# Strassen for the output projection of six token tiles, and a residual added by accumulating DMA

## The chip, the cores and the metric

One core of a Trainium2 chip. The metric is the device time of one execution in microseconds (us). Executions of one kernel lie within about 0.3% of their median, so each time is the median of several. Engines: PE is TensorE, VectorE, ScalarE and GpSimd are the other compute engines, SyncE (SP in the profile) only issues DMAs. The granted clock is the share of TensorE's full clock that its throttle let through.

## The reference, cut to what matters

A linear-attention layer and a gated feed-forward layer, 2048 tokens of width 1024, bf16:

```python
def _A_ref(x, wqkv, wo):                      # attention
    ...                                       # q, k, v; phi; kv, z
    o = num / den                             # "division": numerators over denominators
    return (lambda x, *d: x.transpose(*d))(o, 0, 2, 1, 3).reshape(B, S, D) @ wo   # output projection

h  = x + _A_ref(_layernorm(x, axis=-1), A_wqkv, A_wo)          # the residual that the change moves
h2 = h + _B_ref(_layernorm(h, axis=-1), B_W_gate, B_W_up, B_W_down)
```

The kernel handles tokens in 16 tiles of 128. Only the projection `@ wo` and the `x +` ahead of it are changed.

## The kernel before

A helper records every operation, and a step `t` of the stage projects tile t - 4, computes the numerators of tile t and divides them. The parts that matter:

```python
def a2_div(st):                         # VectorE: division of tile st, 128x1024
    ...                                 # two small operations for 1 / denominator
    PL.add("dve", lambda e: e.tensor_tensor(out=osb[:, k, :]..., in0=nv[:, :, :, 0:Dh], in1=rden[...], op=ALU.mult), ...)
    dma_t(sl_to[kt], oT[:, kt, :, :], osb[:, k, :], "T3d_%d" % st, ...)   # SyncE: DMA transpose for the projection

def a4_mm(st):                          # PE: 16 matmuls, 128x512 each, into one of two bank pairs
    ...
def a4_h(st):                           # VectorE: h = x + projection, then stored by SyncE
    PL.add("dve", lambda e: e.tensor_tensor(out=hsb[:, hs, :], in0=ps[:, b:b + 2, :], in1=x2(st)..., op=ALU.add), ...)
    if TPP <= st and st + NX2 < NST:
        load_x2(st + NX2)
    dma(sl_hs[hs], ov[st * P:(st + 1) * P, :], hsb[:, hs, :], "st_h_%d" % st, ...)
    ...                                 # tiles 0 to 7 (TPP = 8): statistics of the second norm
def a4_norm(st):                        # tiles 0 to 7: ScalarE normalises, SyncE transposes (T5d)
    PL.add("act", lambda e: e.activation(out=xn[:, kx, :], in_=hsb[:, hs, :], func=ACTF.Identity, ...), ...)
    dma_t(sl_tx[kx], hnT[:, :, st * P:(st + 1) * P], xn[:, kx, :], "T5d_%d" % st, ...)

pool_t = t_sums(0, "pool")              # GpSimd: eight 128x512 sums of feed-forward weights
for t in range(NE, NST + LAG + 1):
    if LAG <= t < NST + LAG: a4_mm(t - LAG)
    if t < NST: a2_num(t); a2_div(t)
    if LAG <= t < NST + LAG: a4_h(t - LAG)
    if LAG + 1 <= t < TPP + LAG + 1: a4_norm(t - LAG - 1)
    if t in (5, 7, 18, 19): load_w_next()
    if t >= 9: run(pool_t, 1)
    if 15 <= t < 19: s_sums()[t - 15]()   # VectorE: 128x2048 sums of feed-forward weights
```

Two DMA transposes matter: **T3d**, from the division to the projection of the same tile, and **T5d**, from the second norm to the feed-forward. Both are issued by SyncE, in the order in which the program records them.

Of the kernel before, what the change touches and what calls it, by code (L numbers as in the profile page):

```python
# [6 lines left out]
ALU = mybir.AluOpType  # L7
# [125 lines left out]
def bass_sequential_preLN__linear_attn_block__glu_gated_reglu__prompt_kernel(  # L133
# [15 lines left out]
    _, S, D = A_x.shape  # L149
# [56 lines left out]
    with es:  # L206
# [67 lines left out]

        osb = RE[:, 0:NO * D].rearrange("p (a b) -> p a b", a=NO)
        oT = RE[:, NO * D:(NO + NOT) * D].rearrange("p (a g t) -> p a g t", a=NOT, g=NG)
        ftmp = RE[:, 0:(NO + NOT) * D].bitcast(f32).rearrange("p (a b) -> p a b", b=SBW)
        c22 = RE[:, 2 * D:3 * D].rearrange("p (a b) -> p a b", b=SBW)
        c12 = RE[:, 3 * D:4 * D].rearrange("p (a b) -> p a b", b=SBW)
# [42 lines left out]
        Et = RX[:, 0:NPH * NW].rearrange("p (a b) -> p a b", a=NPH)  # L322
        ajunk = RX[:, 0:D]
        btmp = RX[:, NPH * NW:(NPH + 4) * NW].bitcast(f32).rearrange("p (a b) -> p a b", a=2)

        def TWq(j):
            if j < 2:
# [36 lines left out]
        def slots(name, n):  # L364
            return [_Slot(sem("%s%d" % (name, i))) for i in range(n)]
# [19 lines left out]
        sl_out2 = slots("dou2_", STB)  # L385
        sl_fin = slots("dfin_", STB)
        sl_tx = slots("dtx_", NXN)
        sl_to = slots("dto_", NOT)
        sl_hs = slots("dhs_", NHS)
        sl_hl = slots("dhl_", 2)  # L390
        sl_xl = slots("dxl_", 2)
# [2 lines left out]
        def bufs(name, n):  # L394
            return [_Buf("%s%d" % (name, i)) for i in range(n)]
# [20 lines left out]
        B_dt = bufs("dt_", NDT)  # L416
        B_rd = bufs("rd_", NDT)
        B_oT = bufs("oT_", NOT)
        B_x2 = bufs("x2_", TPP + NX2)
        B_hs = bufs("hs_", NHS)  # L420
        B_hscr = bufs("hscr_", NST)
# [48 lines left out]
        def flat(x):  # L470
            return [b for row in x for b in (flat(row) if isinstance(row, list) else [row])]
# [8 lines left out]
            b_.over = B_TWk  # L480
        for b_ in B_f + B_c22 + B_c12:
            b_.over = B_o + B_oT
        for b_ in B_hl + B_xl:
            b_.over = B_x2[TPP:]
        for b_ in flat(B_T):
            b_.over = B_wq
        for b_ in B_S:
# [23 lines left out]
        for b_ in B_hres + B_ds:  # L511
            b_.over = B_lsum
        for b_ in B_outst:
            b_.over = B_E + B_bt + [B_TWq[2], B_junk]
        for b_ in B_hnE:
            b_.over = B_o + B_oT
        for b_ in B_V:
            b_.over = B_hnE
        for b_ in flat(B_hh) + B_out2:
            b_.over = flat(B_xnT) + flat(B_pqT)  # L520
        for b_ in flat(B_pqT):
            b_.over = flat(B_wkv)
        B_TWq[3].over = [B_zeros]
# [8 lines left out]
        def touch_bank(b):  # L532
            bank_clock[0] += 1
            bank_last[b] = bank_clock[0]
# [33 lines left out]
        def dma_t(slot, dst_ap, src_ap, name, reads=(), writes=()):  # L568
            return PL.add("sp", lambda e: e.dma_start_transpose(dst_ap, src_ap), reads=reads, writes=writes,
                          slot=slot, name=name)  # L570
# [193 lines left out]
        def mm(out_ap, lhsT, rhs, start, stop, reads, bbuf, name, skip=False):  # L764
            return PL.add(
                "pe",
                lambda e: e.matmul(out_ap, lhsT, rhs, start=start, stop=stop, skip_group_check=skip),  # L767
                reads=reads, writes=[bbuf], name=name,
            )
# [433 lines left out]
        NB = [0, 1, 2, 3]  # L1203
        NUW = Dh + 2

        def a2_num(st):
            r, i, t = st // (NST // 2), (st % (NST // 2)) // 2, st % 2
            for b_ in NB:
                touch_bank(b_)
            for g in range(NG):  # L1210
                for h in range(HPG):
                    sl = slice(h * Dh, (h + 1) * Dh)
                    mm(ps[:, NB[h], g * NUW:g * NUW + Dh + 1], pqT[sl, r, t, g, i * P:(i + 1) * P],
                       kvz[sl, g, 0:Dh + 1], True, True, [B_pqT[r][t][g]] + B_kvz, B_bank[NB[h]],
                       "num_%d_%d" % (st, g), skip=True)

        def a2_div(st):
            k = st % NO
            kd = st % NDT
            kt = st % NOT  # L1220
            rb = [B_bank[b_] for b_ in NB]
            nv = ps[:, 0:HPG, 0:NG * NUW].rearrange("p h (g w) -> p g h w", w=NUW)
            PL.add("dve", lambda e: e.tensor_scalar(
                out=dtmp[:, kd, :].rearrange("p (g h) -> p g h", h=HPG), in0=nv[:, :, :, Dh],
                scalar1=1e-6, scalar2=None, op0=ALU.add), reads=rb, writes=[B_dt[kd]], name="dtmp_%d" % st)
            PL.add("dve", lambda e: e.reciprocal(out=rden[:, kd, :], in_=dtmp[:, kd, :]),  # L1226
                   reads=[B_dt[kd]], writes=[B_rd[kd]], name="rden_%d" % st)
            PL.add("dve", lambda e: e.tensor_tensor(  # L1228
                out=osb[:, k, :].rearrange("p (g h e) -> p g h e", h=HPG, e=Dh),
                in0=nv[:, :, :, 0:Dh],  # L1230
                in1=rden[:, kd, :].rearrange("p (g h) -> p g h", h=HPG).unsqueeze(3).to_broadcast([P, NG, HPG, Dh]),
                op=ALU.mult), reads=rb + [B_rd[kd]], writes=[B_o[k]], name="o_%d" % st)
            dma_t(sl_to[kt], oT[:, kt, :, :], osb[:, k, :], "T3d_%d" % st, reads=[B_o[k]], writes=[B_oT[kt]])

        H_PAIRS = [4, 6]

        a4_bank = {}

        def a4_mm(st):
            k = st % NOT  # L1240
            b = a4_bank[st] = min(H_PAIRS, key=lambda b: max(bank_last[b], bank_last[b + 1]))
            for nt in range(ND2):
                touch_bank(b + nt)
                for ct in range(NG):
                    mm(bank(b + nt, NW), oT[:, k, ct, :], wo[:, ct, nt * NW:(nt + 1) * NW],
                       ct == 0, ct == NG - 1, [B_oT[k], B_wo[nt]], B_bank[b + nt], "a4_%d_%d" % (st, nt))

        def a4_h(st):
            xs = x2_slot(st)
            hs = st % NHS  # L1250
            b = a4_bank.pop(st)
            PL.add("dve", lambda e: e.tensor_tensor(out=hsb[:, hs, :], in0=ps[:, b:b + 2, :],  # L1252
                                                    in1=x2(st).rearrange("p (a c) -> p a c", a=2), op=ALU.add),
                   reads=[B_bank[b], B_bank[b + 1], B_x2[xs]], writes=[B_hs[hs]], name="h_%d" % st)
            if TPP <= st and st + NX2 < NST:
                load_x2(st + NX2)
            dma(sl_hs[hs], ov[st * P:(st + 1) * P, :], hsb[:, hs, :], "st_h_%d" % st, reads=[B_hs[hs]],
                writes=[B_hscr[st]])
            if st >= TPP:
                return  # L1260
            ks = st % 2
            a4_k[st] = ks
            src = hsb[:, hs, :]
            junk = ajunk
            for f_ in act_stats(src, [B_hs[hs]], junk, B_junk, s2[:, ks, 0:4], B_s2[ks], "ln2_%d" % st):
                f_()
            m_, r_, n_ = s2[:, ks, 0:1], s2[:, ks, 2:3], s2[:, ks, 4:5]
            PL.add("pool", lambda e: e.tensor_scalar(out=n_, in0=m_, scalar1=r_, scalar2=-1.0, op0=ALU.mult,
                                                     op1=ALU.mult),
                   reads=[B_s2[ks][0], B_s2[ks][2]], writes=[B_s2[ks][4]], name="lnn_%d" % st)  # L1270

        a4_k = {}

# [741 lines left out]
        for p in range(NP_):  # L2015
# [5 lines left out]
            if p + 2 < NP_:  # L2021
# [25 lines left out]
                        twq.pop(0)()  # L2047
                v_group(p + 2, {2: v2, 3: v3, 5: v5, 6: v6})
        assert not twq and not twv and not twk
        for i in range(ND2):  # L2050
            load_wo(i)
        NE = 4
        for r in range(2):
            for ct in range(NG // 2):
                hooks = {}
                if r == 0 and ct == 0:
                    hooks[7] = lambda: kvaccs(NP_ - 1)
                if r == 0 and ct == 1:
                    kvc = kvfin()
                if r == 0 and ct >= 1:  # L2060
                    for h_ in (1, 3, 4, 7):
                        if kvc:
                            hooks[h_] = kvc.pop(0)
                if r == 1:
                    hooks[6] = lambda t=ct: a2_num(t)
                q_group(r, ct, hooks)
                if r == 1:
                    pend[1].insert(2 if ct + 1 < NG // 2 else 0, lambda t=ct: a2_div(t))
                if r == 0 and ct == 0:
                    for i in range(TPP + NX2):  # L2070
                        load_x2(i)
        flush()
        LAG = NOT
        pool_t = t_sums(0, "pool")
        for t in range(NE, NST + LAG + 1):
            if LAG <= t < NST + LAG:
                a4_mm(t - LAG)
            if t < NST:
                a2_num(t)
                a2_div(t)  # L2080
            if LAG <= t < NST + LAG:
                a4_h(t - LAG)
            if LAG + 1 <= t < TPP + LAG + 1:
                a4_norm(t - LAG - 1)
            if t in (5, 7, 18, 19):
                load_w_next()
            if t >= 9:
                run(pool_t, 1)
            if 15 <= t < 19:
                s_sums()[t - 15]()  # L2090
        load_w_next()
        load_w_next()
        for q in range(NWR):
# [158 lines left out]
```

## Time and profile before

| | before |
|---|---|
| median of 3 | 726.51 us (725.54 to 727.18) |
| span in the profile, granted clock | 723.5 us, 1.00 |
| third tile of the stage (tile 2) starts | 177.21 us |
| first feed-forward matmul | 229.75 us |
| the **stretch** between these two | 52.54 us |

(One of the recorded expectations calls the tile at 177.21 us the second; two tiles start before it.) The stretch is the measure by stage that I use below: all that the change can move lies in it or at the program's end, and the first 177 us vary a little from execution to execution. In timelines, columns are start, length, engine, line, operation, and output <- input. Most lines that bound the kernel are in the prediction. One view that it doesn't show is the timeline of SyncE's queue, here for the kernel before; columns are start, length, engine, line, operation, and output <- input. `RE<-RE` is a T3d, `RH<-RXH` a T5d, `out_dram<-RXH` a store.

```profile
208.63 1.30 SPq L569 DMA_TRANSPOSE RH<-RXH  x1
210.04 1.27 SPq L569 DMA_TRANSPOSE RE<-RE  x1
...
213.32 1.29 SPq L569 DMA_TRANSPOSE RH<-RXH  x1
214.72 1.50 SPq L569 DMA_TRANSPOSE RE<-RE  x1
```

Issuing a transpose keeps SyncE for 1.3 us or more, and the entries follow each other almost without a pause. The transposes at 210.04 and 214.72 are those of tiles 12 and 13. Tile 13's division ended at 210.29 (start 209.06, 1.23 us), so its transpose was issued 4.4 us after its data were ready. Direct projection has enough distance (four tiles) to hide that.

### The profile page before, as it was taken

What the parts mean: (1) busy time and instruction counts of PE and PEld (TensorE: products, weight loads), DVE (VectorE), ACT (ScalarE), POOL (GpSimd) and SP (SyncE); (2) the same over time, 40 slices, a digit from 0 to 9 for tenths busy, and PEclk for the clock granted to TensorE, in tenths of its full rate; (3) what the DMA queues carried; (4) which work ended last, traced back from release to release, by engine and by line L of the source; (5) the groups of instructions that cost most, each with busy time, mean ns of one, the idle gap of its engine ahead of it and who ended that gap; (6) DMA issues with size and microseconds to landing.
All of it is one profiled execution on the core that took longest, in us unless ns stands there. A gap on an engine that the chain in (4) does not pass through costs nothing.

```text
span 723.5 us, 12104 instructions
## 1 busy us (share of the span) xinstructions
PE 717.1 (99%) x4521; PEld 384.6 (53%) x4521; DVE 587.2 (81%) x1024; ACT 361.0 (50%) x632; POOL 109.5 (15%) x177
## 2 busy tenths in 40 slices
PE   9999999999999999999999999999999999999998
PEld 4444444344444444444444568865555555547887
DVE  7878867799776889888988787787889877887984
ACT  4878666764841456687757111035455545423010
POOL 1411100000360103322321002310000000000331
PEclk9999999999999999999999999999999999999999
DMA  9652244023998897999999999994555572037996
GB/s 316 207 115 61 37 131 156 13 29 68 195 229 258 245 267 228 281 296 264 326 298 276 302 265 315 320 211 119 149 166 140 158 248 81 1 102 252 315 321 174
DMA packets 192986, 143.59 MB, mean 198 GB/s; under 512 B 51872, under 2 KB 170400, under 8 KB 192928
## 3 DMA queue, kind: packets, MB, share of 16 engines
q1 hardware_dynamic: 188224, 138.50, 66.6%
q0 software_dynamic: 4032, 3.67, 3.6%
q8 instruction: 35, 0.57, 0.3%
q10 hardware_dynamic: 672, 0.66, 0.3%
q14 instruction: 23, 0.19, 0.1%
HBM read 98.76 MB, written 32.51 MB: 181 GB/s over the span
## 4 chain that ended last, share of the span: by engine, by line
PE 89%; DVE 6%; ACT 2%; issue 1%; SPq 1%; DMA 1%; POOL 0%; DVEq 0%; ACTq 0%
PE ps L767 89%; SPq L565 1%; DVE RAB L853 1%; DMA RE<-in_A_x_dram 1%; DVE RE L1228 1%; DVE RX L850 1%; ACT RX L846 1%; DVE RX L1069 1%; ACT RXH L805 1%; DVE RW L963 0%; DVE RWG L988 0%; ACT ps L772 0%; DVE RE L853 0%; DVE rden L1226 0%; DVE RE L1661 0%
## 5 line engine op out<-in xcount | busy, mean ns | idle before, releaser
L772 ACT ACTIVATE ps<-ps 128x512 f32<-128x512 f32 (+1 forms) x192 | 108.8, 567 | 218.0 <-PE ps L767 210.8
L767 PE MATMUL ps<-RC,RO 128*128 128x512 f16 x616 | 143.0, 369 | 0.0
L767 PE MATMUL ps<-RH,RWG 128*128 128x512 bf16 x448 | 108.1, 379 | 0.0
L767 PEld LDWEIGHTS ps<-RC,RO 128*128 128x128 f16 x616 | 60.3, 98 | 63.5
L767 PE MATMUL ps<-RC,RWG 128*128 128x512 f16 x320 | 76.8, 380 | 0.1
L767 PEld LDWEIGHTS ps<-RH,RWG 128*128 128x128 bf16 x448 | 43.8, 98 | 46.9
L767 PE MATMUL ps<-RH,RO 128*128 128x512 bf16 (+1 forms) x256 | 61.2, 379 | 0.0
L1470 DVE TENSOR_TENSOR RAB<-ps,RAB 128x512 bf16<-128x512 f32 x56 | 37.3, 686 | 29.4 <-PE ps L767 29.3
L767 PE MATMUL ps<-RW,RE 128*128 128x512 bf16 x256 | 57.6, 380 | 0.7 <-DVE RXH L1252 0.7
L1670 POOL DMA_DIRECT2D out_dram<-RX x20 | 17.9, 1256 | 263.3 <-DVE RX L1661 221.0
L767 PE MATMUL ps<-RAB 128*128 128x512 bf16 (+2 forms) x270 | 57.1, 351 | 0.1
L767 PE MATMUL ps<-RW,RAB 128*128 128x256 f16 (+3 forms) x362 | 52.9, 301 | 0.0
L767 PEld LDWEIGHTS ps<-RC,RWG 128*128 128x128 bf16 (+1 forms) x320 | 30.0, 98 | 40.0 <-ACT ps L772 6.0
L772 ACT ACTIVATE RE<-ps 128x512 f32<-128x512 f32 (+1 forms) x64 | 31.5, 503 | 37.8 <-PE ps L767 37.8
L767 PEld LDWEIGHTS ps<-RW,RAB 128*128 128x128 f16 (+1 forms) x362 | 35.4, 98 | 14.4 <-DVE RX L1661 0.2
L1354 DVE TENSOR_TENSOR RO<-RWG 128x1024 f16<-128x1024 bf16 x54 | 37.0, 684 | 6.4 <-DMA RWG<-in_B_W_up_dram 4.7
L1661 DVE TENSOR_TENSOR RE<-ps,RE 128x512 f32<-128x512 f32 x44 | 30.2, 687 | 14.3 <-PE ps L767 13.8
L772 ACT ACTIVATE RAB<-ps 128x512 bf16<-128x512 f32 x56 | 33.3, 594 | 16.6 <-PE ps L767 16.3
L767 PEld LDWEIGHTS ps<-RH,RO 128*128 128x128 f16 (+1 forms) x256 | 24.4, 98 | 30.0 <-ACT RX L772 1.6
L1456 DVE TENSOR_TENSOR RAB<-ps,RE 128x512 bf16<-128x512 f32 x56 | 37.1, 685 | 2.8 <-PE ps L767 1.9
L767 PEld LDWEIGHTS ps<-RW,RE 128*128 128x128 bf16 x256 | 24.0, 98 | 28.7 <-DVE RXH L1252 1.2
L1465 ACT ACTIVATE RAB<-RAB 128x1024 bf16<-128x1024 bf16 x28 | 29.5, 1055 | 19.4 <-DVE RAB L1456 18.9
(163 smaller groups left out, 1168.7 us busy)
## 6 DMA issues: line engine op xcount, KB each, us to landing
RWG<-in_B_W_gate_dram SPq DMA_DIRECT2D x28, 512.0 KB, 6.8
RWG<-in_B_W_up_dram SPq DMA_DIRECT2D x28, 512.0 KB, 5.5
RW<-l_scr SPq DMA_DIRECT2D x20, 448.0 KB, 5.8
RW<-in_B_W_down_dram SPq DMA_DIRECT2D x14, 512.0 KB, 5.7
t_scr<-RW SPq DMA_DIRECT2D x14, 512.0 KB, 5.0
l_scr<-RX SPq DMA_DIRECT2D x7, 1024.0 KB, 5.9
RE<-l_scr SPq DMA_DIRECT2D x15, 448.0 KB, 4.5
RE<-in_A_x_dram SPq DMA_DIRECT2D x23, 256.0 KB, 3.3
```

The costliest lines, as they stand in the source:

```text
L565: return PL.add(eng, lambda e: e.dma_start(dst_ap, src_ap), reads=reads, writes=writes, slot=slot, name=name)
L767: lambda e: e.matmul(out_ap, lhsT, rhs, start=start, stop=stop, skip_group_check=skip),
L772: PL.add("act", lambda e: e.activation(out=dst, in_=src, func=func), reads=reads, writes=writes, name=name)
L805: PL.add("act", lambda e: e.activation(out=junk[:, c0:c1], in_=src[:, c0:c1], func=func, scale=scale, accum_out=sv[:, col:col + 1]), reads ...
L846: PL.add("act", lambda e: e.activation(out=Et[:, k, :], in_=src, func=ACTF.Exp), reads=[src_buf], writes=[B_E[k]], name=name + "_exp")
L850: PL.add("dve", lambda e: e.tensor_scalar(out=Et[:, k, :], in0=Et[:, k, :], scalar1=1.0, scalar2=1e-6, op0=ALU.min, op1=ALU.add), reads=[] ...
L1354: PL.add(eng, lambda e: e.tensor_tensor(out=tb(j, u), in0=f0(u), in1=f1(u), op=ALU.subtract), reads=[B_w[i + x] for x in r] + ([B_T[k + x] ...
L1456: PL.add("dve", lambda e: e.tensor_tensor(out=d, in0=src, in1=ftmp[:, u, :], op=ALU.add), reads=[bsrc, B_s5[u]], writes=[db], name=name)
L1465: PL.add("act", lambda e: e.activation(out=d, in_=d, func=ACTF.Relu), reads=[], writes=db, name=name)
L1470: PL.add("dve", lambda e: e.tensor_tensor(out=d, in0=bank(b), in1=d, op=ALU.mult), reads=[B_bank[b]], writes=[db], name=name)
L1661: PL.add(eng, lambda e: e.tensor_tensor(out=dst, in0=in0, in1=in1, op=op), reads=reads, writes=writes, name=name)
L1670: PL.add("pool", lambda e: e.dma_start(dst, src, accum_op=ALU.add), reads=[bsrc], writes=[B_hscr[st]], slot=sl, name="acc_%d_%d" % (st, dh))
```

## The change

Intent: twelve fewer matmuls on the engine that bounds the kernel. Tiles 10 to 15 are projected in three pairs by Strassen's scheme (7 products instead of 8), which needs sums of weights (TWo, four of 128x2048 on VectorE) and of tokens (four of 128x512 per pair, two SBUF inputs each). The residual of tiles 8 to 15 leaves VectorE: the lower half of the output is prefilled with x by one DMA, and the projection is added onto it by accumulating DMAs that GpSimd issues. The core of the diff:

```diff
+        dma(sl_pf[0], ov[TOK:2 * TOK, :], xv[TOK:2 * TOK, :], "fill", writes=B_hscr[TPP:])
...
+        W0 = TPP // 2 + 1
+        def acc_h(st):
+            h_, bh = wo_hs(st)
+            PL.add("pool", lambda e: e.dma_start(ov[st * P:(st + 1) * P, :], h_, accum_op=ALU.add),
+                   reads=[bh], writes=[B_hscr[st]], slot=sl_ac[st - TPP], name="acc_h_%d" % st)
+        def so_sums(p): ...                       # four token sums of a pair, on VectorE
+        def wo_group(p, pool, hooks): ...         # seven products, ScalarE copies, VectorE combinations
...
-            if t >= 9:
-                run(pool_t, 1)
+            if t >= 9:                                   # in step(t)
+                fs.append(lambda: run(pool_t, 1))
+            if 6 <= t < 10:
+                fs.append(lambda: run(two, 1))           # the sums TWo
...
+        for t in range(NE, 2 * W0 + LAG):                # tiles 0 to 9 directly
...
+                if t == 2 * W0 + LAG - 1:
+                    run(sums, 4)                         # token sums of the first pair
+                a4_out(t - LAG)                          # copy out of PSUM, then acc_h
+                a2_div(t)
...
+        for p in range(W0, NST // 2):                    # tiles 10 to 15 in three groups
+            t = 2 * p + 4
+            sm = [lambda: run(sums, 2)]
+            if p == W0:
+                hooks = {3: num(t) + step(t), 5: sm + sm, 6: num(t + 1), 7: step(t + 1)}
+            else:
+                hooks = {3: step(t), 5: sm, 6: sm, 7: step(t + 1)}
+            wo_group(p, [4, 5, 6, 7], hooks)
```

## The prediction

> **What bounds the kernel now.** I read the page first, for the engine that fills the span, then the chain that ended last, then a table by stage, then the matmul timeline of the stage that the change touches.
>
> ```profile
> PE 717.1 (99%) x4521; PEld 384.6 (53%) x4521; DVE 587.2 (81%) x1024; ACT 361.0 (50%) x632; POOL 109.5 (15%) x177
> ...
> PE 89%; DVE 6%; ACT 2%; issue 1%; SPq 1%; DMA 1%; POOL 0%; DVEq 0%; ACTq 0%
> ```
>
> PE (TensorE) is busy for 99% of the span and is 89% of the chain, so only fewer matmuls, or fewer gaps between them, can shorten the program. The granted clock is full throughout (PEclk 9 in all 40 slices). The touched stage, normalisation of the attention output plus output projection, lies at about 169 to 230 us. In the timeline of PE there:
>
> ```profile
> 172.58 3.63 PE L767 MATMUL ps<-RW,RE 128*128 128x512 bf16 x16
> 176.14 0.37 PE L767 MATMUL ps<-kvz,RAB 32*128 32x33 bf16 x32
> 177.21 3.63 PE L767 MATMUL ps<-RW,RE 128*128 128x512 bf16 x16 [0.70 <-DVE RXH L1252]
> 180.77 0.37 PE L767 MATMUL ps<-kvz,RAB 32*128 32x33 bf16 x32
> ...
> 211.98 3.63 PE L767 MATMUL ps<-RW,RE 128*128 128x512 bf16 x16
> 215.54 0.37 PE L767 MATMUL ps<-kvz,RAB 32*128 32x33 bf16 x32
> 215.84 14.07 PE L767 MATMUL ps<-RW,RE 128*128 128x512 bf16 x64
> 229.75 1.89 PE L767 MATMUL ps<-RH,RWG 128*128 128x512 bf16 x8
> ```
>
> One token tile is 16 projection matmuls followed by 32 small numerator matmuls, and starts 3.86 us after the last (177.21 to 181.08). The last four tiles (64 matmuls) take 229.75 - 215.84 = 13.91 us, 0.217 us each. There is one PE gap, 0.70 us at 177.21, made by VectorE's residual add; after it PE never stops. So the stage is PE-bound, with little spare on VectorE. Timeline of VectorE, one tile:
>
> ```profile
> 192.92 0.19 DVE L1223 TENSOR_SCALAR dtmp<-ps 128x32 f32<-128x32 f32 x1 [0.82 <-PE ps L767]
> 193.15 0.35 DVE L1226 RECIPROCAL rden<-dtmp 128x32 f32<-128x32 f32 x1
> 193.60 1.23 DVE L1228 TENSOR_TENSOR RE<-ps,rden 128x1024 bf16<-128x1024 f32 x1
> 194.75 1.22 DVE L1252 TENSOR_TENSOR RXH<-ps,RC 128x1024 bf16<-128x1024 f32 x1
> ```
>
> Division, then residual add, about 3.0 us of each 3.86 us; only 0.82 us is idle. The numerators use one set of four PSUM banks, so the next numerators need this division; the add frees one of only two pairs of projection banks.
>
> **What the Trainium skill says.** (1) "TensorE: Matmul & The Clock Gate", section "Wait — 56ns, not 53.3ns?", gives 215.7 ns from start to start of warm 512-column matmuls; this trace shows 217 (13.91 us / 64), so it agrees. (2) "SBUF — State Buffer", section "SBUF: two separate sides": VectorE instructions with two SBUF inputs and GpSimd instructions that read SBUF exclude each other on a shared port for the whole instruction. The trace before does not test this here: GpSimd's weight sums end at 214.1 us and VectorE's 128x2048 sums begin at 219.24. After the change they can meet. (3) "DMA: Bandwidth & Descriptors", section "SWDGE vs HWDGE vs iDMA": accumulation during a DMA must be issued from GpSimd. This kernel does so in its down projection, where an issue takes 1.2 us of GpSimd (median of line 1670) and lands in 6.7 us.
>
> **The change part by part.**
> *Removed from PE.* Six tiles are three pairs. A pair costs 32 matmuls directly, 7 products of 4 = 28 by Strassen, all still 128x512. So 3 x 4 = 12 matmuls go: 12 x 0.217 = **2.6 us, the ceiling of the gain**, 0.36% of 726.5 us.
> *Moved off the path anyway.* The residual of the last eight tiles: eight VectorE adds of 1.22 us become one VectorE copy of the same size, two ScalarE copies, and Strassen's combinations. Three loads of x and five later ones (256 KB each) become one fill of the output's lower half (2 MB read, 2 MB written, DRAM to DRAM) ahead of the output weights on SP's queue. In the timeline of SP the last transpose of the first part begins by 92 us, the weights are issued at 101.55 and first used at 168.73; the page gives 0 or 2 tenths of DMA in the slices about 126 to 145 us. I expect the fill to be invisible. The accumulating writes are first read back in feed-forward unit 2, some 25 us after the stage (units are 12.1 us), against a landing of 6.7 us: also hidden.
> *Added to VectorE.* Four weight sums of 128x2048 at steps 6 to 9 (1.22 us each in the same operation earlier, line 963; 1.13 from start to start); twelve token sums of 128x512, 0.42 us (line 988, about 0.34 apart); six combinations with a PSUM input, 0.69 us. Against 8.5 us removed that is 4.5 + 4.1 + 4.1, net 4 us more, which matters only where VectorE is short.
> *Cost one, the weight sums.* A step becomes 2.96 + 1.13 = 4.1 us of VectorE against 3.86 us of PE. Using the trace's idle 0.64 to 0.82 us per step, VectorE is late by 0.2, 0.6, 0.9 and 1.1 us after the four. The add has about 0.6 us of slack before PE wants its banks (add of tile 4 ends 192.10, banks taken 192.66). So PE loses about 0.5 us in steps 10 to 12.
> *Cost two, the Strassen groups.* A group has only banks 4 to 7. Its chain is P1, ScalarE copy into a second bank (0.58 us), P6 on top, copy again, P5, and a bank comes back only after VectorE's combination. P7 (0.87 us) just hides the 0.2 us delay plus the copy: in the query groups, the same chain on four banks, matmul quadruples start 0.86 to 0.90 us apart instead of 0.87, so about 0.1 us per group. Group 5 asks more: VectorE must do two divisions (1.76 each), two combinations, four token sums and one 128x2048 sum, 3.5 + 1.4 + 1.4 + 1.15 = 7.4 us, in 28 x 0.217 + 2 x 0.3 = 6.7 us of PE. The combination that frees bank b comes behind the token sums, so group 6's first copy, then its P6, comes about 0.4 us late. ScalarE reaches group 5 with the last norm (ends near 208.8 us before the change) and two copies in front: another 0.5 us. Division 15 ends about 10.3 us into the groups; its transpose lands 3.0 to 5.8 us later (median 3.9 in this window) at about 14.3, where group 6's token sums want it near 13.4; they hold up the combination behind them, and group 7's P6 loses about 0.7 us. Sum for the groups: 0.3 + 0.5 + 0.4 + 0.7 = 1.9 us if all come true; half of it is guess, so I take 1.0.
> *Sum.* 2.6 - 0.5 - 1.0 = 1.1 us gained: 726.5 - 1.1 = **725.4 us**.
>
> **The rivals.** (a) *Full gain*: the group hooks place VectorE's work so that nothing on PE waits. For it: the key and value groups of the same form ran from 39 to 128 us on the chain as one unbroken PE piece (488 matmuls). Against it: they had five banks, not four, and no division in between. Result 723.9. (b) *VectorE becomes the bound*, made worse by the shared port: GpSimd's eight sums of 1.15 us and its DMA issues now run beside the two-SBUF-input sums; each meeting could add up to 1.15 us. It would cancel the gain: 726.5 to 727.5. (c) *Transfers in the way*: the transpose of tile 15 queues behind accumulates and weight loads (DMA share in 177 to 200 us is already 1.03). At 5.8 us instead of 3.9 it costs 2 us more: about 727. Speaking against it, eight ordinary stores, eight loads of x and the last norm transposes leave the same stretch. (d) *The fill delays the weights or x*: only if 2 MB took over 60 us, which at the 350 GB/s seen near 110 us it cannot.
>
> **Range and chances.** The scatter of the three runs before is 1.6 us, as large as the effect. Ceiling 723.9; all costs together with one long transpose, 727. Range 723.8 to 727.0. Two per cent is 14.5 us, five times the ceiling, and no listed loss is near it: faster 0.01, same 0.98, slower 0.01.
>
> **What would show each step right or wrong.** Matmuls 4521 minus about 12; projection matmuls on oT fall from 256 to 160, plus 84 in groups. The first feed-forward matmul, at 229.75 us before, should start at about 228.6: under 227.5 means rival (a), over 229.7 means (b) or (c). PE idle should appear near 200 us behind the residual add, and inside groups 6 and 7 behind the PSUM copies. Token sums waiting on a transpose would show (c); sums much longer than 0.42 or 1.22 us would show the port. Everything after 240 us should keep its length. The prediction is wrong if the fill stalls the start of the stage, or if the later stages shift by more than the stage gained.

## The result, and the profile after

The changed kernel takes **736.75 us** (median of 4, 735.02 to 738.65) against 726.2 for the kernel before (median of 4). The ratio is 1.0145, interval [1.0115, 1.0174]. A ratio is the mean time of one kernel's fast runs over that of the other's of the same rounds, so it isn't quite the quotient of the medians. The kernel is within 2%, as predicted, but on the wrong side: 10.5 us slower, far above the range's 727.0.

From the page of the kernel after, engines and chain:

```profile
PE 717.2 (98%) x4509; PEld 382.9 (52%) x4509; DVE 597.4 (81%) x1039; ACT 372.2 (51%) x652; POOL 115.5 (16%) x185
...
PE 83%; DVE 8%; DMA 3%; ACT 3%; issue 2%; SPq 1%; POOL 0%; DVEq 0%; ACTq 0%
```

Exactly twelve matmuls are gone, yet PE's busy time is the same to 0.1 us: the remaining ones took longer somewhere. PE's share of the chain fell from 89 to 83%, and 9.8 us were added to the span (733.3). The first feed-forward matmul starts at 239.19, and from there to the end both kernels take 494 us, so nearly all of it was lost in the stretch: 61.58 us (177.61 to 239.19) against 52.54, 9.0 us more. Adding the 2.6 us that the missing matmuls save, 11.6 us went somewhere. The matmul timeline of the kernel after shows most of it; a bracket gives the idle time before a row and who ended it:

```profile
209.16 1.04 PE L785 MATMUL ps<-RW,RAB 128*128 128x512 bf16 x4
215.19 3.60 PE L785 MATMUL ps<-RAB 128*128 128x512 f16 x8 [4.99 <-DVE RAB L1324]
...
225.15 1.04 PE L785 MATMUL ps<-RAB 128*128 128x512 f16 x4 [0.35 <-ACT ps L790]
...
229.52 1.03 PE L785 MATMUL ps<-RW,RE 128*128 128x512 bf16 x4
233.27 1.04 PE L785 MATMUL ps<-RAB 128*128 128x512 f16 x4 [2.73 <-DVE RAB L1324]
234.82 1.04 PE L785 MATMUL ps<-RAB 128*128 128x512 f16 x4 [0.51 <-ACT ps L790]
...
239.19 1.03 PE L785 MATMUL ps<-RH,RWG 128*128 128x512 bf16 x4
```

Two gaps, 4.99 and 2.73 us, both ended by a token sum (L1324), and two small ones, 0.86 us together. Besides, the eight matmuls at 215.19 took 3.60 us where eight later ones take 1.89. The windows view of the same stretch says why; the column before the last two is the granted clock:

```profile
209.00:210.20 1.20, 1.20 (x36) 0.43 (x24) 0.00 (x0) 1.20 (x2) 1.20 (x2) 1.00 1.09 213
210.20:215.00 4.80, 0.00 (x0) 0.00 (x0) 4.13 (x1) 1.09 (x3) 4.64 (x5) 0.69 1.03 189
...
216.00:217.00 1.00, 1.00 (x4) 0.43 (x3) 0.86 (x4) 0.00 (x0) 0.00 (x0) 0.50 1.23 204
...
219.00:222.00 3.00, 3.00 (x60) 1.36 (x44) 2.17 (x4) 1.66 (x3) 0.00 (x0) 1.00 0.83 93
```

During the gap the clock fell (1.00 in 211.5 to 212.0 us, 0.50 in 212.0 to 212.5), and it stayed at half until 218.8. The Trainium skill, "TensorE: Matmul & The Clock Gate", Part 1, says that an idle window of about 3.4 us halves the clock and a busy window of about the same length restores it. The return agrees: PE works again from 215.19 us, and 3.6 us later the clock is full. The fall does not: it came 1.8 us after the last matmul before the gap, and in the 3.4 us before it (208.6 to 212.0) PE had been busy for 1.60 us. The half clock cost 1.7 us more (3.60 - 1.89). In the second row one VectorE instruction fills 4.13 of 4.80 us: a single token sum. The chain of the kernel after has it, with the transposes that precede the two gaps (the first is that of tile 11, issued 4.5 us after its division ended at 203.27; the second that of tile 15):

```profile
207.74 3.11 DMA RAB<-RE
...
210.87 4.27 DVE RAB L1324
...
226.28 6.48 DMA RE<-RE
```

And what GpSimd did meanwhile (its timeline; L1480 is a weight sum, L1310 the issue of an accumulating DMA):

```profile
210.30 1.42 POOL L1480 TENSOR_TENSOR RO<-RWG,RO 128x512 f16<-128x512 bf16 x1
211.39 1.16 POOL L1310 DMA_DIRECT2D out_dram<-RE  x1
212.01 2.83 POOL L1480 TENSOR_TENSOR RO<-RWG 128x512 f16<-128x512 bf16 x2
```

The token sum starts 0.57 us after GpSimd's and ends at 215.14, 0.30 us after GpSimd's last sum (214.84). The other token sums of this kernel take 0.42 us.

Last, the DMA issues between 195 and 236 us of the kernel after (a group, its count, KB each where it is given, and the median us from issue to landing):

```profile
out_dram<-RE POOLq DMA_DIRECT2D x4, 256.0 KB, 5.6
...
RAB<-RE SPq DMA_TRANSPOSE x4, 3.8
RE<-RE SPq DMA_TRANSPOSE x4, 5.1
```

The first transposes (tiles 8 to 11, `RAB<-RE`) land in 3.8 us; those of tiles 12 to 15 in 5.1, but this median hides two kinds. The transposes of tiles 12 and 15, issued with accumulating DMAs in flight, took 6.62 and 6.48 us, and the second gap waits on the last one; those of tiles 13 and 14, with none in flight, took 3.75 and 3.09.

The sum of what the trace shows: gaps 4.99 + 2.73 + 0.86, half clock 1.71, and 0.68 us ahead of it in the steps with the sums TWo (the tile at 201.45 starts that much later than six periods of 3.86 us after 177.61; 0.28 of it waited for a transpose): 10.97 of 11.6 us. I did not break down the rest.

### The profile page after: what moved, and what is told of

It reads as the page before. It is cut to its first block, busy times and chain, and to the rows that moved or that the text cites. A ratio compares the mean times of both kernels' runs of the same rounds, so it can differ in the third digit from the quotient of the medians.

```text
span 733.3 us, 12108 instructions
## 1 busy us (share of the span) xinstructions
PE 717.2 (98%) x4509; PEld 382.9 (52%) x4509; DVE 597.4 (81%) x1039; ACT 372.2 (51%) x652; POOL 115.5 (16%) x185
## 4 chain that ended last, share of the span: by engine, by line
PE 83%; DVE 8%; DMA 3%; ACT 3%; issue 2%; SPq 1%; POOL 0%; DVEq 0%; ACTq 0%
PE ps L785 83%; DVE RE L1251 1%; SPq L583 1%; DVE RAB L871 1%; DMA RAB<-RE 1%; DMA RE<-in_A_x_dram 1%; DMA RE<-RE 1%; DVE RAB L1324 1%; ACT RX L864 1%; DVE RXH L1278 1%; DVE RX L868 1%; ACT RXH L823 1%; ACT ps L790 1%; DVE RX L1087 1%; DVE rden L1249 0%
## 5 line engine op out<-in xcount | busy, mean ns | idle before, releaser
L790 ACT ACTIVATE ps<-ps 128x512 f32<-128x512 f32 (+1 forms) x198 | 112.3, 567 | 207.0 <-PE ps L785 191.2
L785 PE MATMUL ps<-RAB 128*128 128x512 bf16 (+3 forms) x310 | 68.7, 362 | 8.7 <-DVE RAB L1324 7.7
L785 PE MATMUL ps<-RW,RAB 128*128 128x256 f16 (+3 forms) x414 | 65.3, 311 | 0.3 <-DMA RAB<-RE 0.3
L790 ACT ACTIVATE RE<-ps 128x512 f32<-128x512 f32 (+2 forms) x68 | 33.8, 508 | 38.4 <-PE ps L785 38.4
L785 PEld LDWEIGHTS ps<-RAB 128*128 128x128 bf16 (+1 forms) x310 | 29.8, 99 | 39.7 <-DVE RAB L1324 8.7
L785 PEld LDWEIGHTS ps<-RW,RAB 128*128 128x128 f16 (+1 forms) x414 | 39.9, 98 | 20.1 <-ACT RX L790 0.6
L790 ACT ACTIVATE RAB<-ps 128x512 bf16<-128x512 f32 x56 | 33.3, 595 | 16.8 <-PE ps L785 16.6
L790 ACT ACTIVATE RX<-ps 128x512 f32<-128x512 f32 (+1 forms) x43 | 25.4, 598 | 29.5 <-PE ps L785 29.3
L1480 DVE TENSOR_TENSOR RO<-RWG 128x1024 f16<-128x1024 bf16 x54 | 36.8, 682 | 0.9 <-DMA RWG<-in_B_W_up_dram 0.9
```

Source lines behind the costliest of these rows:

```text
L785: lambda e: e.matmul(out_ap, lhsT, rhs, start=start, stop=stop, skip_group_check=skip),
L790: PL.add("act", lambda e: e.activation(out=dst, in_=src, func=func), reads=reads, writes=writes, name=name)
L1480: PL.add(eng, lambda e: e.tensor_tensor(out=tb(j, u), in0=f0(u), in1=f1(u), op=ALU.subtract), reads=[B_w[i + x] for x in r] + ([B_T[k + x] ...
```

## The experiments

Theories (E came up after e11):
- **A.** GpSimd's weight sums lock VectorE's token sums out of a shared port. A rival, put in e2: GpSimd's DMA issues do.
- **B.** The token sums are late only because tile 11's transpose lands late (a rival of A).
- **C.** The loads of feed-forward weights on SyncE's queue slow the transposes (a rival of D).
- **D.** The accumulating DMAs slow the transposes.
- **E.** SyncE issues the transposes too late, behind others.

All edits are to the changed kernel unless another is named. The stretch is from each run's profile (before: 52.54, changed: 61.58).

| run | median us | ratio to before, interval | stretch |
|---|---|---|---|
| e1_pool_early | 736.45 | 1.0145 [1.0127, 1.0164] | 62.60 |
| e2_acc_late | 731.90 | 1.0080 [1.0065, 1.0095] | 57.59 |
| e3_loads_late | 737.03 | 1.0152 [1.0137, 1.0167] | 63.30 |
| e4_direct_acc | 730.64 | 1.0064 [1.0047, 1.0081] | 55.44 |
| e8_tsum_dve | 733.49 | 1.0109 [1.0092, 1.0126] | 59.63 |
| e9_plain_pool (wrong on purpose) | 733.45 | 1.0106 [1.0091, 1.0121] | 59.94 |
| e10_acc_end | 737.00 | 1.0150 [1.0135, 1.0165] | 63.68 |
| e11_acc_end_tsum_dve | 733.93 | 1.0112 [1.0094, 1.0130] | 59.22 |
| e12_held | 732.20 | 1.0086 [1.0073, 1.0100] | 59.23 |
| e13_held_tsum_dve | 728.02 | 1.0030 [1.0016, 1.0044] | 55.76 |
| e14_direct_held | 725.96 | 0.9998 [0.9983, 1.0013] | 53.48 |
| e15_two_pairs_held | 728.51 | 1.0031 [1.0019, 1.0044] | 53.76 |
| e16_t5d_late | 725.23 | 0.9991 [0.9977, 1.0004] | 52.23 |
| e17_reordered | 725.10 | 0.9988 [0.9974, 1.0002] | 51.94 |
| e18_reordered_two_pairs | 724.36 | 0.9979 [0.9966, 0.9991] | 50.98 |
| e19_direct_acc_again | 730.79 | 1.0065 [1.0050, 1.0080] | 58.21 |
| e20_direct_held_again | 726.02 | 1.0003 [0.9987, 1.0020] | 53.00 |
| e21_direct_plain (wrong on purpose) | 726.37 | 1.0006 [0.9991, 1.0021] | 53.25 |

The medians of the kernel before in these rounds were 725.65 to 726.1.

### Cause A: GpSimd's sums beside VectorE's

**e1_pool_early** runs the weight sums two at a time from step 9 on, to have them done before the token sums.

```diff
-                fs.append(lambda: run(pool_t, 1))
+                fs.append(lambda: run(pool_t, 2))
```

> GpSimd's eight weight sums are issued two per step instead of one, so that all are over before VectorE starts the first token sums (about 210.9 us in the changed kernel). Theory A (the first token sum, 4.26 us instead of 0.42, was held off by GpSimd's back-to-back sums on a shared port, and the 5 us gap then halved TensorE's clock for 3.5 us): the first token sum takes 0.4 us, the 4.99 us gap shrinks to about 1.2 us, the clock stays full, and the program gains 4 to 5.5 us: about 731 to 732.5. Rival B (the sums are late only because the transpose of tile 11 lands at 210.9): the gap stays above 4 us and the time at 736 to 737.

A failed edit: the last two sums stand behind an accumulating DMA's issue on the same engine and still ran from 211.69 to 214.21, the four token sums took 4.79 us, and the gap was 4.72. Inconclusive, and a hint: moving an operation in the program does not clear a window if its engine is held by something else.

**e8_tsum_dve** takes the sums off GpSimd altogether, to VectorE as four of 128x1024.

```diff
-        pool_t = t_sums(0, "pool")
+        pool_t = t_sums(0)
...
-            if t >= 9:
-                fs.append(lambda: run(pool_t, 1))
...
+                if p == NST // 2 - 1:
+                    hooks[4] = [lambda: run(pool_t, 2)]
```

> GpSimd's eight weight sums (1.15 us each) become VectorE's four of 128x1024 (0.69 us), two in the last group and two after it, so GpSimd only issues accumulating DMAs while token sums run. (The run that issued the sums two per step did not clear the window: GpSimd was still summing at 211.7 to 214.2 us, so it decided nothing.) Theory A (shared port, weight sums): the first token sum falls from 4.26 us to 0.4 to 1.6, the first gap from 4.99 to under 2 us, the clock stays full: about 730 to 732. If the weight sums do not matter: 735 or more.

VectorE's timeline of this run:

```profile
210.64 1.68 DVE L1324 TENSOR_TENSOR RAB<-RAB 128x512 f16<-128x512 bf16 x4 [2.63 <-DMA RAB<-RE]
```

Four token sums in 1.68 us, 0.42 each, with the accumulating DMAs' issues still on GpSimd; PE's first gap fell from 4.99 to 1.05 us and the eight matmuls after it took 1.91. So without GpSimd's weight sums there is no 4.26 us, and neither its DMA issues alone nor a late transpose (B) makes it. That the sums alone don't make it either is shown by e2, e10 and e12 below. The time fell only to 733.49, above the expected 730 to 732: the transposes of tiles 12 and 15, beside accumulating DMAs, still took 8.3 and 6.0 us.

The Trainium skill, "SBUF — State Buffer", section "SBUF: two separate sides", says that a VectorE instruction with two SBUF inputs and a GpSimd instruction that reads SBUF exclude each other for a whole instruction, and whoever starts first has the port. The direction agrees. The size in the changed kernel does not follow from one instruction: VectorE was not let in between GpSimd's sums, but only after the last. Where no DMA issue stands among these sums (e12 below), it is let in after each, which fits the page.

### Cause D: accumulating DMAs beside transposes, and its rivals

**e3_loads_late** puts the four loads of feed-forward weights behind the groups (rival C).

```diff
-            if t in (5, 7, 17, 19):
+            if t in (5, 7):
...
-        load_w_next()
-        load_w_next()
+        for _ in range(4):
+            load_w_next()
```

> The two feed-forward weight loads issued between the last groups move behind the last group. Theory C (the transpose of tile 15 takes 6.48 us from issue to landing because four weight loads of 512 KB are issued right behind it): the landing falls to 3 to 4 us, group 7's wait of 2.73 us to about 0, the time to about 733.5 to 734.5. If the loads do not matter, the landing stays above 6 us and the time at 736 to 737. The loads themselves come a few us later; feed-forward unit 1 needs them 12 us after the stage, so no new wait is expected.

737.03 us, and the last transpose still took 6.8 us with a gap of 3.03 behind it. But this edit failed too. SyncE had already issued the loads behind tile 15's transpose in the changed kernel (from 227.72 us, transpose 226.28), and it still does (from 228.05, transpose 226.63). C falls by e13 below instead: there the same four loads follow that transpose (223.66) from 224.95 on, and it lands in 3.16 us.

**e2_acc_late** places the accumulating DMAs of tiles 8 and 9 behind the last group in GpSimd's program.

```diff
         def acc_h(st):
+            if st < 10:
+                acc_hold.append(st)
+                return
+            acc_now(st)
...
         run(pool_t, 8)
+        for st_ in acc_hold:
+            acc_now(st_)
```

> The accumulating DMAs of tiles 8 and 9, issued by GpSimd at 209.4 and 211.4 us, are issued after the last group instead; GpSimd's weight sums stay where they are. If GpSimd's DMA issue[...] is what held the first token sum off, the sum falls to below 1 us and the time to about 732. If it was the weight sums (theory A), the first token sum still takes 2 to 4 us and the time is 734 to 737.

731.9 us, and the first token sum took 0.93 us, with GpSimd's weight sums still in place: what was expected if the DMA issues hold it off, and not if the sums do. The token-sum gap became 0.86 + 1.64, and the clock stayed at 1.0. The T3d of tiles 12 to 15 fell to 3.1 to 4.0 us as well, so the edit touches A and D at once.

**e9_plain_pool** keeps all issues and lets GpSimd's DMAs store instead of accumulate. Its output is wrong, which doesn't matter for the time. (Relative error 0.45.)

```diff
-            PL.add("pool", lambda e: e.dma_start(ov[st * P:(st + 1) * P, :], h_, accum_op=ALU.add),
+            PL.add("pool", lambda e: e.dma_start(ov[st * P:(st + 1) * P, :], h_),
```

> Wrong result on purpose: the eight DMAs of the residual part are issued by GpSimd at the same places and sizes but store plainly instead of accumulating. Theory D (the accumulation[...] makes the DMA transposes beside it take 5.3 to 8.5 us instead of 3.1 to 4): transposes fall to about 4 us, group 7's gap from 2.7 to about 0.5 us, while the first gap stays at 4 to 5 us: 733 to 734.5. If it is any GpSimd-issued DMA beside them, transposes stay above 5 us and the time at 736 to 737.

733.45 us: 0.39 points, some 2.8 us, gained by a plain store of the same bytes. The second gap fell from 2.73 to 1.00, while the first, which is A's, stayed at 4.49.

**e10_acc_end** and **e11_acc_end_tsum_dve** put all eight accumulating DMAs at the end of GpSimd's program (e11 on top of e8).

```diff
-            if st < 10:
+            if st >= TPP:
```

> All eight accumulating DMAs are issued after the last group; weight sums stay on GpSimd. Theory D: no transpose above 4.8 us, group 7's gap under 1.3 us. Theory A: the token sums are still held off by weight sums, some 2.5 us of gap remains in group 5. About 730 to 731.5.

> Both: accumulating DMAs after the last group and weight sums on VectorE, so that GpSimd does nothing in the group stage. If A and D are the whole cause, what is left are the costs of the prediction (weight sums of the projection 0.7 us, late transposes of tiles 11 and 15, about 1 us each): 725 to 727.5. If it stays above 729, a third cause is missing.

e11 failed as an edit: GpSimd, with nothing else left to do, reached the DMAs early and issued each as soon as its data was ready (at the same times as in e8, 224.39 us for one of them). e10 worked in part: the first two went out behind the weight sums, at 215.68 and 216.51 us instead of 209.44 and 211.39. The first token sum then took 0.47 us, but the transposes of tiles 13 and 14, now beside these two, took 6.39 and 5.17. In time the two runs equal e8 and the changed kernel.

**e12_held** therefore makes each accumulating DMA also wait for the last matmul of the last group.

```diff
+                   deps=[PL.prog["pe"][-1]],
                    reads=[bh], writes=[B_hscr[st]], slot=sl_ac[st - TPP], name="acc_h_%d" % st)
```

> The run that moved the accumulating DMAs to the end of GpSimd's program did not delay them: nothing stood before them in GpSimd's queue, so they still went out as soon as their data was ready. Here each also waits for the last matmul of the last group, so none is in flight beside a transpose of the stage; weight sums stay on GpSimd. Theory D (accumulating DMAs lengthen the transposes): every transpose of the stage lands in 3 to 4.8 us, and the group 7 gap falls to under 1 us. Theory A: the token sums of group 5 still take 2 to 4 us in place of 1.4. Time 729 to 731.5. If transposes stay above 5 us, D is wrong.

732.2 us, above the expected range. All transposes of the groups took 3.1 to 3.9 us and the second gap was gone. The token sums still met GpSimd's sums (gaps 1.97 + 1.63 + 1.15), but in another way than in the changed kernel. VectorE's timeline, GpSimd's (L1485 is a weight sum) and a row of PE's:

```profile
211.04 4.59 DVE L1329 TENSOR_TENSOR RAB<-RAB 128x512 f16<-128x512 bf16 x4 [3.25 <-DMA RAB<-RE]
```

```profile
210.33 2.44 POOL L1485 TENSOR_TENSOR RO<-RWG 128x512 f16<-128x512 bf16 x2
212.73 2.62 POOL L1485 TENSOR_TENSOR RO<-RWG,RO 128x512 f16<-128x512 bf16 x2
```

```profile
214.49 1.87 PE L785 MATMUL ps<-RAB 128*128 128x512 f16 x4 [1.63 <-DVE RAB L1329]
```

With no DMA issue among GpSimd's sums, the two engines take turns: the four token sums take 0.72, 1.37, 1.26 and 1.26 us, and GpSimd's sums 1.33 instead of 1.15. e2 (0.93, 1.37, 1.26, 0.42) and e10 (0.47, 1.37, 1.26, 1.26) show the same. Where DMA issues stand before or between the sums, the first token sum took 4.26 us (changed kernel), 3.53 (e1), 3.31 (e3) and 4.72 (e9, plain stores); with the issues alone 0.43 (e8). So A is shown for the two together: weight sums and DMA issues of GpSimd, mixed, keep VectorE out until the last sum. Why, no run shows. The last row has four matmuls in 1.87 us instead of 1.04: the clock was at half from 212.8 to 223.0 us.

**e13_held_tsum_dve** does both, e12 and e8.

> The same, with the weight sums on VectorE (two in the last group, two after it): GpSimd does nothing beside the groups. A and D together: the first token sum 0.4 us, transposes 3 to 4.8 us, 727 to 729.5. What is left over the kernel before is then the plain lateness of the transposes of tiles 11, 13 and 15 on SP's queue, plus the cost of the projection's weight sums.

728.02 us. PE idles as long in this run's stretch as in e12's (5.8 us in both, by the windows view); the 3.5 us between the two stretches are the half clock, under which e12 ran 7.45 us of matmuls and e13 none. By ratios, without A the loss of 1.45% falls by 0.36 points, without D by 0.59, without both by 1.15 points (8.3 us of 726). The two overlap: as long as one is there, it covers part of what the other's removal gains.

**The residual part alone.** e4_direct_acc projects all 16 tiles directly and keeps the prefill and the accumulating DMAs. e14_direct_held is the same with e12's wait.

```diff
-        W0 = TPP // 2 + 1
+        W0 = NST // 2
```

> The residual part alone: all sixteen tiles projected directly (256 matmuls), no Strassen sums, the last eight residuals added by the accumulating DMA onto the prefilled output. If the residual part is free, as predicted, the time is that of the kernel before, 725.5 to 727, and the first feed-forward matmul starts within 0.6 us of 229.75. If the accumulating DMAs or the fill cost something by themselves, it is 728 or more.

> The residual part alone (no Strassen), accumulating DMAs held until the last projection matmul. With them in flight this form took 730.64 us, with transposes of 7.0 to 8.5 us and a 2.48 us wait on them. Theory D: transposes back to 3 to 4.8 us, that wait gone, 725.3 to 726.5, equal to the kernel before. If the fill or another part of the residual change cost the 4.8 us, it stays at 729 or more.

730.64 against 725.96 us. But the profiled execution of e4 was 2.6 us late at tile 2 already (180.05; one of the program's first loads of x had landed in 5.9 us, in e19 in 3.4), so by stage it showed less than by time. I took both again on one chip, with a third that stores plainly (e9's edit).

> The residual part alone, once more. If the late start belonged to that execution, the second tile starts near 177.5 us (180.05 then), and the time is 728 to 730; the stretch from there to the feed-forward's first matmul (52.5 us before the change, 55.4 then) is again over 54.5 us, with transposes of over 6 us, if the accumulating DMAs are what lengthens it. If the start is the kernel's own, it is late again and the time is 730 to 731.

> The same with the accumulating DMAs held to the end, once more: 725.5 to 726.5 us, the stretch 52.5 to 53.5 us, transposes 3 to 5 us.

> The residual part alone with plain stores from GpSimd in place of accumulating ones (wrong result on purpose). If the accumulation is what slows the transposes, they take 3 to 5 us and the stretch is under 53.7 us; if any writes from GpSimd do it, it is as long as in the run with accumulation.

The start had belonged to that execution: 177.49 us this time. Time and stage now agree. Accumulating: 730.79 us, stretch 58.21. Held back: 726.02 and 53.00. Plain stores: 726.37 and 53.25. PE's timeline of e19, then the landing of the T3d in 195 to 232 us, of e19, e20 and e21 in this order:

```profile
220.19 2.65 PE L785 MATMUL ps<-RW,RE 128*128 128x512 bf16 x6 [3.23 <-DMA RE<-RE]
```

```profile
DMA to landing us min/median/max: 3.1/4.4/8.1
```

```profile
DMA to landing us min/median/max: 3.1/3.6/4.9
```

```profile
DMA to landing us min/median/max: 3.2/4.2/6.6
```

The T5d took up to 8.9, 4.2 and 7.1 us. D is shown, and it costs 4.8 us by itself (730.79 - 726.02). About 1.6 of them are again the half clock, behind the gap of 3.23 us: 3.18 us of matmuls ran at 0.50. By time, 4.4 us come from accumulating rather than storing (730.79 - 726.37; no execution of one comes near the other's). By landing the difference is smaller, and the 3 to 5 us expected of e21 were missed: its worst T3d took 6.6 us. PE waited only 0.52 us for it, in part because it was issued earlier (210.41 us, in e19 212.08). The eight VectorE adds that the residual part takes away are worth nothing by themselves: held back, this kernel is the kernel before to within 0.1% (0.9998 and 1.0003). The Trainium skill, "DMA: Bandwidth & Descriptors", section "Issuing engines are not separate DMA queues", says that DMAs from all engines run on the same 16 DMA engines and interleave; the runs agree in that GpSimd's DMAs delay SyncE's. Why an accumulating one delays a transpose more than a store of the same size does, no run here shows.

### Cause E: the order on SyncE's queue

e13 left 1.9 us over the kernel before and 4.5 over what twelve matmuls should give. Its PE timeline:

```profile
212.05 1.91 PE L785 MATMUL ps<-RAB 128*128 128x512 f16 x8 [2.00 <-DVE RAB L1329]
215.12 0.37 PE L785 MATMUL ps<-kvz,RAB 32*128 32x33 bf16 x32 [1.17 <-DVE RE L1251]
...
222.53 1.04 PE L785 MATMUL ps<-RAB 128*128 128x512 f16 x4 [1.34 <-ACT ps L790]
```

The token sums at the first gap wait for the transpose of tile 11. Its division ended at 203.16, and SyncE's queue in e13 has it (`RAB<-RE`) here:

```profile
206.55 1.29 SPq L587 DMA_TRANSPOSE RH<-RXH  x1
207.89 1.51 SPq L587 DMA_TRANSPOSE RAB<-RE  x1
```

It is issued 4.7 us late, directly behind a norm's transpose. (The chain names the division running at 207.8 as what released it, but that one is tile 12's: a releaser is inferred, and the queue's own timeline is the better witness.) **e16_t5d_late** emits each T5d two steps later, so the T3d go first; nothing else differs from e13.

```diff
-            dma_t(sl_tx[kx], hnT[:, :, st * P:(st + 1) * P], xn[:, kx, :], "T5d_%d" % st, ...)   # in a4_norm
+            if 0 <= t - 7 < TPP:                                                                # in step(t)
+                fs.append(lambda: t5d(t - 7))
```

> As the held run with the weight sums on VectorE (728.0 us), but the norms' transposes are issued two steps later on SyncE, so that the token tiles' transposes go first. If lateness on SyncE's queue is the remainder, the PE gaps of 2.00 and 1.17 us at the token sums shrink to under 0.6 us together and the time is 725.5 to 727. If it is VectorE's order, the time stays within 0.5 us of 728.0.

**725.23 us**, 2.8 less than e13. SyncE's queue and PE's waits in the stretch:

```profile
203.28 1.90 SPq L587 DMA_TRANSPOSE RAB<-RE  x1
...
207.95 1.23 SPq L587 DMA_TRANSPOSE RE<-RE  x1
```

```profile
PE ps L785 <- ACT ps L790: 1.1, 2, 0.8
PE ps L785 <- DVE RXH L1278: 0.9, 2, 0.7
```

The transpose of tile 11 is issued 0.14 us after its division, that of tile 12 at once, and all PE waits on token sums are gone. E is shown: it accounts for e13's loss against the kernel before, and for 2.8 of the 4.5 us. The 0.7 in the second row is the gap that the kernel before has too; a wait of 0.78 on ScalarE, behind the last norm and two copies out of PSUM at the start of the first group, is what the prediction had named there.

### VectorE's order, and fewer pairs

**e17_reordered** is e16 with the sums TWo spread over steps 6, 8, 10 and 12, and each pair's token sums behind the last combination of the group before; the feed-forward sums move into and behind the last group.

```diff
-            if 6 <= t < 10:
+            if t in (6, 8, 10, 12):
...
-                hooks = {3: num(t) + step(t), 5: sm + sm, 6: num(t + 1), 7: step(t + 1)}
+                hooks = {3: num(t) + step(t), 6: num(t + 1)[0:1] + s4 + num(t + 1)[1:], 7: step(t + 1)}
```

> As the run before, and VectorE's projection weight sums come in four later steps and each pair's token sums after the last combination of the group before. If VectorE's order is the remainder, the time falls to 723.6 to 725.5 us, under the kernel before; if not, it stays where the run before is, and a gap at the token sums takes the place of the one at the combinations.

725.10 us: no difference from e16. The early loss disappeared (eight periods of 3.86 us from 178.18 to 209.09, without a gap), but the first group then waited 1.59 us for ScalarE (`ACT ps L790`) instead of 0.78. In both runs the copies that this product needs stand behind the norm of the last tile and two copies out of PSUM. So VectorE's order is not what was left, as far as the time shows.

**e15_two_pairs_held** (on e12, weight sums still on GpSimd, TWo spread) and **e18_reordered_two_pairs** (on e17) use two pairs.

```diff
-        W0 = TPP // 2 + 1
+        W0 = TPP // 2 + 2
```

> Candidate: two pairs (tiles 12 to 15) by Strassen instead of three, accumulating DMAs held, the four projection weight sums at every second step. 8 matmuls saved = 1.7 us. GpSimd's weight sums should be over (about 215) before the token sums (216), and no transpose should be late. 724.3 to 726. If SP's lateness still bites, 726 to 728.

> The same order with two pairs instead of three: 8 matmuls saved instead of 12, 0.87 us less gain at most, but transposes have longer to arrive. Where order is the remainder, 724.6 to 726 us; where each pair costs what it costs in the held runs, it lies near 727 to 728.

e15 took 728.51 us (its profiled execution, 726.76, was its fastest, so its stretch flatters it), no better than three pairs in e13. e18 took **724.36 us**, ratio 0.9979 [0.9966, 0.9991]: the only version that is faster than the kernel before, if barely. PE's waits in its stretch are one line, the old gap:

```profile
PE ps L785 <- DVE RXH L1278: 0.7, 1, 0.7
```

Eight matmuls fewer are worth 8 x 0.217 = 1.74 us; e18 has 1.4 of them (725.77 - 724.36). With no new wait, Strassen pays what its matmuls say, and no more.

## Why the prediction was wrong

- **What bounds the kernel, and the ceiling of the gain: right.** PE lost exactly 12 matmuls, and where nothing new waits (e18) a matmul less is worth what was said.
- **"I expect the fill to be invisible": right** as far as the time shows. It landed 8.8 us after its issue at 92.09 us. Residual part with DMAs held back: 0.9998 and 1.0003.
- **"The accumulating writes are first read back in feed-forward unit 2 ... also hidden": this step failed.** I asked when their data was needed, not what they share the DMA engines with while in flight. They lengthened the transposes beside them: 4.8 us by themselves (e19 against e20). Rival (c) did name the transpose of tile 15 behind "accumulates and weight loads", at 2 us, and was near it there (6.48 us to land, a gap of 2.73); it missed tile 12 (6.62). What it set against itself, "eight ordinary stores, eight loads of x and the last norm transposes leave the same stretch", was in part misread: all eight norm transposes stay (the last at 213.32 us before, 213.36 after), only five of the loads were there, and a store and an accumulation of the same bytes are not the same thing here (e21 against e19).
- **Rival (b), "each meeting could add up to 1.15 us": the mechanism was right, the size wrong.** The term was one GpSimd sum, and that is what a meeting costs while the two take turns (1.26 to 1.37 instead of 0.42 us in e12). With DMA issues among the sums, one token sum took 4.26 us, waiting for GpSimd's whole run. The sum was wrong as well: eight meetings of 1.15 us are 9.2, and the rival's range had room for 3.6 (723.9 to 727.5). Behind the gap so made the clock fell, for 1.7 us more. The prediction had no term for the clock.
- **Cost one, the sums TWo, "about 0.5 us": right** (0.68 measured, 0.28 of it behind a transpose; gone in e17, where they are spread out). Its way there, late by 0.2 to 1.1 us, isn't what 4.1 against 3.86 us a step gives (0.24 to 0.96).
- **Cost two, "I take 1.0": the step was mis-sized, in one term.** The ScalarE waits inside the groups were of the predicted kind and size (0.35 and 0.51, and 0.78 in e16). But I put each transpose's issue at the end of its division, and did not ask for tiles 10 and 11 at all, which the first group's token sums need. SyncE's queue was the reason: 4.5 us late for tile 11 in the changed kernel, 4.7 in e13, 2.8 us of time (e13 against e16). The kernel before already showed it, at 214.72.
- **Range.** It added small costs of waits known beforehand. The loss came from three resources, each off the critical path before: the port of VectorE and GpSimd, the DMA engines, and SyncE's queue. None of them was given a term over 2 us. And the upper end, "all costs together with one long transpose, 727", is short of its own terms: 723.9 + 0.5 + 1.9 + 2 = 728.3.

What stays open: why e16 and e17, with three pairs, keep only 0.5 to 0.7 of the 2.6 us. PE idles for 1.6 us in their stretches, and ScalarE's wait at the start of the first group is the largest piece in their traces (0.8 and 1.6 us). No run removed it.

## What to carry to other kernels

Before moving work off the critical path, list what it shares with the path: a port, the DMA engines, an issuing queue; "its result is needed late" says nothing of that. Look at when a transfer is issued, not only at how long it takes, and give transfers that PE waits for the front of the queue. When an experiment shows little, check in its trace that the edit did what it should (e1, e3 and e11 did not, e10 only in part), and compare by stage as well as by time.

## What the Trainium skill lacked or had wrong

- "SBUF — State Buffer": it speaks of a lock for one instruction. That fits while GpSimd only sums (a 128x512 VectorE sum took up to 1.37 us instead of 0.42, the two taking turns). With DMA issues among GpSimd's sums it took 4.26 us, past three sums. The page does not say that such a mixed run of GpSimd can keep VectorE out until its end.
- "DMA: Bandwidth & Descriptors": it says who may issue an accumulating DMA, but not what one costs beside other transfers. Beside them the T3d took up to 8.1 us (4.9 with none in flight, 6.6 beside plain stores of the same size), and the kernel 4.8 us more.
- "DMA: Bandwidth & Descriptors", section "Issuing engines are not separate DMA queues": the time to initiate a DMA is called usually small relative to the DMA itself. A transpose kept SyncE for about 1.3 us against 3.1 us or more to land, and at two transposes and a store for each tile of 3.86 us the queue ran 4.7 us behind; reordering it alone gained 2.8 us.
- "TensorE: Matmul & The Clock Gate", Part 1, ties the fall of the clock to an idle window of about 3.4 us. Here it fell without one: 1.8 us into the gap of the changed kernel, in or just after gaps of 2.88 (e1), 3.03 (e3) and 3.23 us (e19), after one of 1.97 (e12), and after 1.15 and 1.43 us with matmuls between them (e11). In e13, gaps of 2.00 and 1.17 us left it at 1.00. How much idle time is enough, no run shows. The return is as the page has it: 3.6 us after PE resumed.
